# Moving LayerNorm tiles within SBUF by four transfers on one counter, in place of a round trip through DRAM, under a new order list

## The chip, the cores and the metric

The kernel runs on one core of a Trainium2 chip. The core has five engines with a queue of instructions each: TensorE (PE in the profile; its weight loads have a row of their own, PEld), VectorE (DVE), ScalarE (ACT), GpSimd (POOL) and SyncE (SP), which here only issues DMA transfers. The metric is the device time of one execution in microseconds, median of several runs; less is better.

## The reference, cut to what matters

Two transformer layers with shared weights on x of shape (1, 2048, 512) in bf16. Each layer is a sliding-window attention block and an MLP block, both with a LayerNorm in front and a residual behind:

```python
def _A_ref(x, wqkv, wo):                      # H = 32 heads of Dh = 16, window W = 256
    qkv = (x @ wqkv).reshape(B, S, 3, H, Dh).transpose(2, 0, 3, 1, 4)
    q, k, v = qkv[0], qkv[1], qkv[2]
    scores = einsum("bhqd,bhkd->bhqk", q, k) * (Dh ** -0.5)
    scores = where((i - j >= 0) & (i - j < W), scores, -1e9)
    return einsum("bhqk,bhkd->bhqd", softmax(scores), v) ... @ wo
def _B_ref(x, w1, b1, w2, b2):                # F = 1792
    return gelu_tanh(x @ w1 + b1) @ w2 + b2
for _ in range(2):
    x = x + _A_ref(_layernorm(x), wqkv, wo)
    x = x + _B_ref(_layernorm(x), w1, b1, w2, b2)
```

## The kernel before, in words

**Tiling.** The 2048 rows are 16 tiles of 128 rows; with the two layers there are 32 tiles, tau = 0 to 31. X stays in SBUF for the whole kernel. Attention works on blocks of two tiles (16 blocks, `attention(b, ...)`): scores of a block are computed in visits of 512 columns into four PSUM banks (line 944), ACT takes the exponential of them into the ring `E` (line 948), DVE or POOL multiplies the triangular parts with a mask (line 969), PE multiplies with V (line 1031), DVE transposes and scales the sums (lines 1034 to 1046), and PE applies Wo (`outproj`). The MLP works on ten jobs of two or four tiles (`mlp`, line 1091): W1 for 14 chunks of F, gelu on ACT (lines 1106 and 1114), W2, and the residual (line 790).

**LayerNorm and the transposed rows.** `layernorm` (line 727) computes the normalised rows of a tile on DVE and POOL (lines 734 to 747). PE needs them with the model dimension on the partitions. For early and for the last tiles, PE transposes them through PSUM (line 768). For 44 of the 64 LayerNorm tiles (`by_dma`: those in front of attention from tau = 14 on, those in front of the MLP from tau = 4 to 29) it goes another way: DVE transposes in blocks of 32 x 32 into one of four buffers `xs_` (line 753), SP writes that buffer to a scratch tensor `scr` in DRAM (line 758), and when that has landed, SP reads it back in another order into the destination (line 760): `xnTA` (18 tiles, read by the projections to Q, K and V) or `xnTB` (26 tiles, read by W1). Each transfer moves 128 KB; eight scratch buffers are used in turn.

**What sets the order.** Every operation is recorded as a node by `add` (line 200) with its engine, its reads and writes. `ORDER` is a list of all nodes, written out, found in advance by a search; `TURNS` says which engine takes an operation that two engines could do, `BANKS` which PSUM banks it gets. `_List.run` goes through `ORDER`, with planned durations; those of the two transfers are at lines 756 to 761. `_Sched.op` (line 89) then gives each operation its semaphore waits, and `emit` (line 164) writes each engine's instructions in the order of the list. So every engine runs a fixed queue. SP's queue holds the first loads, the 88 transfers of the LayerNorm tiles and the 17 stores of the result; a transfer that waits holds up all behind it. A transfer is counted on one of 16 DMA counters, used in turn; a transfer adds 16 to it when it has landed, and may be issued only when the counter's last one has landed (line 102).

Of the kernel before, what the change touches and what calls it, by code (L numbers as in the profile page):

```python
# [6 lines left out]
dt = mybir.dt  # L7
# [48 lines left out]
class _Sched:  # L56
# [32 lines left out]
    def op(self, eng, fn, reads=(), writes=(), inc=1, dma=False, start=0.0, end=0.0, n=1, joins=(), behind=None):  # L89
# [7 lines left out]
        counter = eng  # L97
        if dma:
            counter = "dma%d" % (self.dma_rr % self.N_DMA_SEMS)
            self.dma_rr += 1  # L100
            inc = 16
            need(counter, self.cnt_val[counter])
# [12 lines left out]
        waits = sorted(req.items(), key=lambda x: -self.when[x])  # L115
# [12 lines left out]
        self.prog[eng].append(dict(fn=fn, waits=waits, counter=counter, inc=inc, start=start, n=n))  # L128
# [35 lines left out]
    def emit(self):  # L164
        nc = self.nc
        self.spread()
        with nc.Block() as block:
            for eng in self.ENGINES:
                prog = self.prog[eng]

                def run(e, _prog=prog, _pe=eng == "pe"):
                    for o in _prog:
                        if _pe:
                            r = o["fn"](_Slots(e, o["at"]))
                        else:
                            for c, v in o["waits"]:
                                e.wait_ge(self.cnt_sem[c], v)
                            if o["fn"] is None:
                                continue
                            r = o["fn"](e)  # L180
                        r.then_inc(self.cnt_sem[o["counter"]], o["inc"])
# [4 lines left out]
class _List:  # L186
# [13 lines left out]
    def add(self, eng, fn, dur, reads=(), writes=(), prio=0.0, alloc=(), free=(), after=(), geo=None, table=None,  # L200
            issue=0.0, alt=(), war=(), lock=False, joins=()):
# [17 lines left out]
        if eng == "pe":  # L219
# [6 lines left out]
            issue=issue, lock=lock, alts=((eng, fn, dur),) + tuple(alt), n=n, behind=None,  # L226
# [72 lines left out]
def bass_interleave_layers__sliding_block__dense_activation_gelu__prompt_kernel(  # L299
# [44 lines left out]
    NSC = 8  # L344
# [30 lines left out]
    with ExitStack() as kctx:  # L375
        S_ = _Sched(nc, kctx)

        def sb(name, shape, dtype=dt.bfloat16):
# [20 lines left out]
        scr = nc.dram_tensor("scr_x", (NSC, P, D), dt.bfloat16, kind="Internal").ap()  # L399
# [811 lines left out]
```

## Time and profile before

| what | us |
|---|---|
| three runs, median | 448.97 (448.90 to 451.24) |
| the profiled execution's own time | 449.14 |
| its span, first to last instruction | 447.4 |
| PE, ACT, DVE, POOL busy | 425.2, 386.4, 373.5, 239.9 |

The profile is of one execution; its span is 1.7 us shorter than its time. An engine is busy while one of its instructions runs; matmuls are pipelined, so that two that overlap count once and a busy PE need not be at its peak. A "wait" is idle time of an engine and is put down to what ended it. DMA-issuing instructions are not busy time; for them the profile tells the time from issue to landing.

### The profile page before, as it was taken

What the parts mean: (1) busy time and instruction counts of PE and PEld (TensorE: products, weight loads), DVE (VectorE), ACT (ScalarE), POOL (GpSimd) and SP (SyncE); (2) the same over time, 40 slices, a digit from 0 to 9 for tenths busy, and PEclk for the clock granted to TensorE, in tenths of its full rate; (3) what the DMA queues carried; (4) which work ended last, traced back from release to release, by engine and by line L of the source; (5) the groups of instructions that cost most, each with busy time, mean ns of one, the idle gap of its engine ahead of it and who ended that gap; (6) DMA issues with size and microseconds to landing.
All of it is one profiled execution on the core that took longest, in us unless ns stands there. A gap on an engine that the chain in (4) does not pass through costs nothing.

```text
span 447.4 us, 19245 instructions
## 1 busy us (share of the span) xinstructions
PE 425.2 (95%) x8691; PEld 232.2 (52%) x8764; DVE 373.5 (83%) x745; ACT 386.4 (86%) x458; POOL 239.9 (54%) x301
## 2 busy tenths in 40 slices
PE   8999999888999999999999999999999999999997
PEld 5555655645544545545445445445454454545665
DVE  6999989899998989888999898998898876775512
ACT  2999999999999998899997999889979999892452
POOL 4764786755865357643356457672455454444330
DMA  9920000001120112010220101301031003002021
GB/s 264 370 88 4 4 1 3 5 3 50 43 56 13 50 51 75 25 37 16 68 67 3 39 24 50 74 15 49 27 85 50 15 5 94 22 8 62 0 84 48
DMA packets 39903, 22.88 MB, mean 51 GB/s; under 512 B 24460, under 2 KB 39308, under 8 KB 39820
## 3 DMA queue, kind: packets, MB, share of 16 engines
q1 hardware_dynamic: 39404, 21.24, 16.4%
q8 instruction: 69, 1.13, 1.0%
q10 hardware_dynamic: 416, 0.39, 0.3%
q14 instruction: 14, 0.11, 0.1%
HBM read 13.77 MB, written 7.86 MB: 48 GB/s over the span
## 4 chain that ended last, share of the span: by engine, by line
PE 70%; ACT 15%; DVE 10%; issue 2%; DMA 2%; POOL 0%
PE ps L32 69%; ACT E L948 10%; ACT gT L1114 2%; ACT gT L1106 2%; DVE TT L1034 2%; DVE E L969 1%; DMA xnTB<-scr_x 1%; DVE stat L734 1%; DVE QT L720 1%; ACT L948 1%; DVE X L790 1%; DVE xs_ L753 1%; DMA scr_x<-xs_ 1%; DVE Va L720 1%; DVE OT L1044 1%
## 5 line engine op out<-in xcount | busy, mean ns | idle before, releaser
L948 ACT ACTIVATE E<-ps 128x1024 bf16<-128x1024 f32 x304 | 285.7, 1044 | 23.9 <-PE ps L32 23.0
L969 POOL TENSOR_TENSOR E<-E,mask 128x512 bf16<-128x512 bf16 (+1 forms) x130 | 134.8, 1052 | 89.9 <-DVE E L969 40.8
L32 PE MATMUL ps<-xnTB,W_sb 128*128 128x512 bf16 (+1 forms) x560 | 115.2, 337 | 1.4 <-issue 0.3
L32 PE MATMUL ps<-W_sb,gT 128*128 128x512 bf16 (+1 forms) x421 | 108.4, 373 | 4.3 <-issue 3.0
L32 PE MATMUL ps<-xnTA,Wqkv_sb 128*128 128x256 bf16 (+1 forms) x544 | 74.6, 267 | 1.5 <-ACT E L948 0.7
L32 PEld LDWEIGHTS ps<-xnTB,W_sb 128*128 128x128 bf16 x560 | 51.6, 98 | 42.9 <-ACT E L948 3.8
L32 PE MATMUL ps<-QT,KT 32*64 32x320 bf16 (+4 forms) x2976 | 65.5, 258 | 4.0 <-ACT E L948 2.0
L790 DVE TENSOR_TENSOR X<-X,ps 128x512 bf16<-128x512 bf16 x63 | 42.4, 676 | 25.3 <-PE ps L32 25.0
L32 PEld LDWEIGHTS ps<-W_sb,gT 128*128 128x128 bf16 x462 | 41.5, 98 | 42.2 <-issue 6.7
L1114 ACT ACTIVATE gT<-ps,b1T 128x512 bf16<-128x512 f32 (+1 forms) x84 | 45.7, 598 | 20.1 <-PE ps L32 19.8
L32 PEld LDWEIGHTS ps<-xnTA,Wqkv_sb 128*128 128x128 bf16 x544 | 47.0, 98 | 24.2 <-ACT E L948 3.5
L32 PEld LDWEIGHTS ps<-QT,KT 32*64 32x64 bf16 x2976 | 27.6, 103 | 51.0 <-ACT E L948 32.5
L969 DVE TENSOR_TENSOR E<-E,mask 128x512 bf16<-128x512 bf16 (+1 forms) x132 | 49.1, 402 | 3.0 <-ACT E L948 3.0
L741 POOL TENSOR_TENSOR statmv<-statmv,mhalf 128x1 f32<-128x1 f32 x64 | 36.6, 575 | 22.8 <-DVE statmv L738 18.9
L32 PE MATMUL ps<-E,Va 64*17 64x128 bf16 (+3 forms) x3872 | 46.0, 229 | 2.5 <-ACT E L948 0.9
L1034 DVE STREAM_TRANSPOSE TT<-ps 128x1024 f32<-128x1024 f32 x32 | 39.8, 1244 | 9.4 <-PE ps L32 9.1
L32 PEld LDWEIGHTS ps<-E,Va 64*17 64x17 bf16 x3872 | 36.7, 85 | 19.5 <-PE ps L32 8.0
L1039 POOL TENSOR_TENSOR TM<-TT,Rc 128x512 bf16<-128x512 f32 x22 | 23.3, 1058 | 44.0 <-DVE E L969 17.8
L734 DVE BATCH_NORM_STATS2 stat<-X 128x6 f32<-128x512 bf16 x64 | 43.0, 678 | 2.7 <-DMA X<-in_A_x_dram 2.4
L1078 POOL TENSOR_TENSOR X<-X,b2b 128x512 bf16<-128x512 bf16 x32 | 36.7, 1157 | 13.2 <-DVE E L969 5.7
L1103 DVE TENSOR_SCALAR gT<-ps,b1T 128x512 bf16<-128x512 f32 (+1 forms) x56 | 35.5, 643 | 8.0 <-PE ps L32 7.7
L864 DVE TENSOR_TENSOR KT<-ps,parmask 128x1024 bf16<-128x1024 f32 x30 | 36.2, 1210 | 2.7 <-PE ps L32 2.5
(56 smaller groups left out, 348.5 us busy)
## 6 DMA issues: line engine op xcount, KB each, us to landing
scr_x<-xs_ SPq DMA_DIRECT2D x44, 128.0 KB, 1.9
W_sb<-in_B_w_dram SPq DMA_DIRECT2D x2, 1792.0 KB, 15.4
xnTB<-scr_x SPq DMA_DIRECT2D x26, 128.0 KB, 2.7
xnTA<-scr_x SPq DMA_DIRECT2D x18, 128.0 KB, 2.7
out_dram<-X SPq DMA_DIRECT2D x15, 128.0 KB, 1.8
Wqkv_sb<-in_A_wqkv_dram SPq DMA_DIRECT2D x4, 256.0 KB, 4.9
X<-in_A_x_dram SPq DMA_DIRECT2D x1, 1024.0 KB, 9.2
Wqkv_sb<-in_A_wqkv_dram SPq DMA_DIRECT2D x1, 512.0 KB, 6.4
```

The source lines that it names most:

```text
L32: return self.e.matmul(*a, **k)
L734: add("dve", lambda e, B: e.bn_stats(stat6[:, k6, :], X[:, t, :]), 590, reads=["X%d" % t], writes=["st%d" % k6], prio=prio)
L741: add("pool", lambda e, B: e.tensor_tensor(out=statmv[:, k, 1:2], in0=statmv[:, k, 1:2], in1=mhalf[:], op=ALU.pow), 535, reads=["ve%d" % k ...
L790: add("dve", lambda e, B: e.tensor_tensor(out=X[:, t, :], in0=X[:, t, :], in1=ps[:, B[g][0], :], op=ALU.add), d_psum(512), reads=["X%d" % ...
L864: add("dve", lambda e, B, g=g, i=i: e.tensor_tensor(out=KT[:, kb, :, 2 * i : 2 * i + 2, :].rearrange("p a c q -> p a (c q)"), in0=ps[:, B[ ...
L948: add("act", lambda e, B, g_=g_, gi=gi: e.activation(E[:, 2 * gi : 2 * gi + 2, e0 : e0 + 512], ps[:, B[g_][0] : B[g_][0] + 2, :], AF.Exp, ...
L969: op = lambda e, B, Ew=Ew, Mw=Mw: e.tensor_tensor(out=Ew, in0=Ew, in1=Mw, op=ALU.mult)
L1034: add("dve", lambda e, B: e.transpose(TT[:, s].rearrange("p a c q d -> p a (c q d)"), ps[:, B[g][0] : B[g][0] + 2, :].rearrange("p a n -> ...
L1039: mul = lambda e, B: e.tensor_tensor(out=TM[:, sm].rearrange("p c q a d -> p a (c q) d"), in0=TT[:, s, :, :, :, 0:Dh].rearrange("p a c q d ...
L1078: add("pool", lambda e, B: e.tensor_tensor(out=X[:, t, :], in0=X[:, t, :], in1=b2b[:], op=ALU.add), 1110, reads=["X%d" % t, "b2b"], writes ...
L1103: add("dve", lambda e, B, g=g, fc=fc: e.tensor_scalar(out=gT[:, fc, 0:M], in0=ps[:, B[g][0], 0:M], scalar1=b1T[:, fc : fc + 1], scalar2=No ...
L1114: add("act", lambda e, B, g=g, fc=fc: e.activation(gT[:, fc, 0:M], ps[:, B[g][0], 0:M], AF.Gelu_apprx_tanh, bias=b1T[:, fc : fc + 1], scal ...
```

## The change

For the 44 tiles the two transfers by way of DRAM become four transfers from SBUF to SBUF. Each takes 32 partitions of `xs_`, 32 KB, and writes 256 bytes to each of the 128 partitions of the destination. All four are issued one after another by SP and count on the same counter, which thereby rises by 64; the scratch tensor is gone. A node of the list can now consist of several transfers (`parts`).

```diff
@@ layernorm @@
-                flat = scr[v].rearrange("p c -> (p c)")
-                room = 0.0 if tau < 12 else 700.0
-                dma(lambda e, B: e.dma_start(scr[v], xs_[:, z, :]),
-                    ["scr%d_0" % v], reads=["xs%d" % z], prio=prio, dur=2200.0 + room, issue=400.0)
-                dma(lambda e, B: e.dma_start(dst.rearrange("p r d j -> p r (d j)"), flat.rearrange("(r p c) -> p r c", r=4, p=P)),
-                    [dname], reads=["scr%d_0" % v], prio=prio, dur=2700.0 + 2 * room, issue=400.0)
+                def move(e, B):
+                    return [e.dma_start(dst[:, r].rearrange("p d j -> p (d j)"), xs_[32 * r : 32 * r + 32, z, :].rearrange("i (q c) -> i q c", q=4))
+                            for r in range(4)]
+
+                dma(move, [dname], reads=["xs%d" % z], prio=prio, dur=4500.0, issue=1600.0, parts=4)
@@ _Sched.op @@
-            inc = 16
+            inc = 16 * parts
@@ _Sched.emit @@
-                        r.then_inc(self.cnt_sem[o["counter"]], o["inc"])
+                        for x in r if isinstance(r, list) else [r]:
+                            x.then_inc(self.cnt_sem[o["counter"]], o["inc"] // o["parts"])
```

`ORDER`, `TURNS` and `BANKS` are replaced as a whole. The new list has 3219 nodes in place of 3263. What can be counted in the two lists: PE issues 8766 matmuls in both, and changes between its three kinds of matmul (128 rows, scores, attention times V) 362 times before and 364 times after; ACT loads 18 tables in both, and the exponentials stand in the same groups between the gelus (44, 24, 50, 34, 1, 39, 40, 40 and 32). ACT takes over three copies of Q, two of V, one to `xnTA` and one to `xv`, and gives one to `xnTB` to DVE. Eight mask operations, three scalings of the attention's sums and one small operation move from POOL to DVE. SP issues 176 transfers for the LayerNorm tiles in place of 88.

More of the change, by code (lines that the diff above doesn't have):

```diff
@@ L87, in _acquire, with op @@
         return True
-    def op(self, eng, fn, reads=(), writes=(), inc=1, dma=False, start=0.0, end=0.0, n=1, joins=(), behind=None):
+    def op(self, eng, fn, reads=(), writes=(), inc=1, dma=False, start=0.0, end=0.0, n=1, joins=(), behind=None, parts=1):
         kn = self.know[eng]
@@ L127, in op @@
             self.res_r[wr] = {}
-        self.prog[eng].append(dict(fn=fn, waits=waits, counter=counter, inc=inc, start=start, n=n))
+        self.prog[eng].append(dict(fn=fn, waits=waits, counter=counter, inc=inc, start=start, n=n, parts=parts))
         return counter, val
@@ L200, in add @@
     def add(self, eng, fn, dur, reads=(), writes=(), prio=0.0, alloc=(), free=(), after=(), geo=None, table=None,
-            issue=0.0, alt=(), war=(), lock=False, joins=()):
+            issue=0.0, alt=(), war=(), lock=False, joins=(), parts=1):
         i = len(self.nodes)
@@ L225, in add @@
             jdeps=frozenset(self.lw[r] for r in joins), alloc=alloc, free=tuple(free), deps=deps, geo=geo, table=table,
-            issue=issue, lock=lock, alts=((eng, fn, dur),) + tuple(alt), n=n, behind=None,
+            issue=issue, lock=lock, alts=((eng, fn, dur),) + tuple(alt), n=n, behind=None, parts=parts,
             heavy=any(a[0] == "pool" and a[2] > 600.0 for a in ((eng, fn, dur),) + tuple(alt)),
@@ L343, in bass_interleave_layers__sliding_block__dense_activation_gelu__prompt_kernel @@
     NXV = 1
-    NSC = 8
     LN_DMA = 14
@@ L398, in bass_interleave_layers__sliding_block__dense_activation_gelu__prompt_kernel @@
         b1raw = xv[0:FC, 0, 0, :]
-        scr = nc.dram_tensor("scr_x", (NSC, P, D), dt.bfloat16, kind="Internal").ap()
         xnTA = sb("xnTA", [P, 2, 2, DC * P])
@@ L680, in bass_interleave_layers__sliding_block__dense_activation_gelu__prompt_kernel, with dma @@
             add("pe", clear(n), took, reads=["zero", "g0"], writes=["ps:init0", "ps:init1"], prio=-200, geo="f")
-        def dma(fn, writes, reads=(), dur=2200.0, prio=0.0, issue=640.0, eng="sp"):
-            add(eng, fn, dur, reads=reads, writes=writes, prio=prio, issue=issue)
+        def dma(fn, writes, reads=(), dur=2200.0, prio=0.0, issue=640.0, eng="sp", parts=1):
+            add(eng, fn, dur, reads=reads, writes=writes, prio=prio, issue=issue, parts=parts)
         queued = {"sp": 0, "act": 0}
@@ L750, in layernorm @@
                 z = xs_rr[0] % NXS
-                v = xs_rr[0] % NSC
                 xs_rr[0] += 1
@@ L1179, in bass_interleave_layers__sliding_block__dense_activation_gelu__prompt_kernel @@
             marks[i] = S_.op(nd["eng"], lambda e, fn=nd["fn"]: fn(e, B), reads=phys(nd["reads"]), writes=phys(nd["writes"]), dma=nd["issue"] > 0,
-                  start=nd["start"], end=nd["vis"], n=n, joins=nd["joins"], behind=marks[nd["behind"]])
+                  start=nd["start"], end=nd["vis"], n=n, joins=nd["joins"], behind=marks[nd["behind"]], parts=nd["parts"])
         S_.wait_all_dma("sp")
```

419 rows, old and new, of tables (BANKS, ORDER, TURNS) are left out of this document.

## The prediction

> **What bounds the kernel now.** I read the page's first part, then the table of stages, the waits, and last the transfers with SP's timeline.
>
> ```profile
> span 447.4 us, 19245 instructions
> PE 425.2 (95%) x8691; PEld 232.2 (52%) x8764; DVE 373.5 (83%) x745; ACT 386.4 (86%) x458; POOL 239.9 (54%) x301
> ```
>
> The share hides two regimes; the stages tell them apart.
>
> ```profile
> 13.00:49.00 36.00, 32.59 (x789) 18.64 (x792) 34.42 (x72) 35.42 (x39) 23.64 (x34) 1.00 0.37 126
> ...
> 85.00:124.00 39.00, 35.27 (x889) 21.04 (x892) 36.63 (x73) 38.61 (x47) 26.67 (x29) 1.00 0.11 30
> 124.00:160.00 36.00, 35.38 (x742) 17.54 (x753) 33.07 (x68) 35.15 (x41) 16.77 (x21) 1.00 0.14 36
> 160.00:200.00 40.00, 39.00 (x840) 20.58 (x829) 34.76 (x69) 36.27 (x42) 26.03 (x33) 1.00 0.17 45
> 200.00:240.00 40.00, 38.94 (x763) 19.70 (x770) 36.64 (x74) 36.60 (x42) 16.72 (x19) 1.00 0.19 49
> 240.00:285.00 45.00, 43.43 (x1001) 22.23 (x1010) 41.07 (x84) 42.64 (x49) 27.62 (x37) 1.00 0.14 37
> 285.00:320.00 35.00, 33.94 (x596) 17.27 (x585) 31.82 (x60) 31.84 (x39) 17.55 (x23) 1.00 0.14 37
> 320.00:360.00 40.00, 38.87 (x816) 20.82 (x823) 34.26 (x62) 36.05 (x42) 20.49 (x21) 1.00 0.17 45
> 360.00:400.00 40.00, 38.90 (x857) 19.03 (x864) 30.52 (x57) 35.56 (x39) 17.39 (x21) 1.00 0.13 36
> ```
>
> The columns are length, then PE, PEld, DVE, ACT, POOL busy, the granted clock, the DMA share and GB/s. From 13 to 124 us ACT is all but full (35.42 of 36, 38.61 of 39) and PE waits. From 124 to 400 us it is the other way round: PE lacks only 0.62 + 1.00 + 1.06 + 1.57 + 1.06 + 1.13 + 1.10 = 7.5 us, ACT about a tenth. The first LayerNorm tile that a transfer moves is transposed at 100 us, so the change works where PE sets the pace, and 7.5 us is the most that filling PE's visible idle time could give there.
>
> ```profile
> PEld ps L32 <- ACT E L948: 46.9, 130, 0.8
> ...
> PEld ps L32 <- DMA xnTB<-scr_x: 0.8, 1, 0.8
> ```
>
> In the waits of all engines a transfer holds up the weight loads once, for 0.8 us; the banks that the exponentials empty do so 130 times. The transfers are nearly hidden already.
>
> **The change part by part.** *Removed: the write to DRAM and the read back.*
>
> ```profile
> L758 SPq DMA_DIRECT2D scr_x<-xs_ x44: 319/332/914, 100.7 to 407.9; - x44
> ...
> scr_x<-xs_ SPq DMA_DIRECT2D x44, 128.0 KB, 1.9
> ...
> xnTB<-scr_x SPq DMA_DIRECT2D x26, 128.0 KB, 2.7
> xnTA<-scr_x SPq DMA_DIRECT2D x18, 128.0 KB, 2.7
> ...
> out_dram<-X SPq DMA_DIRECT2D x2, 64.0 KB, 1.5
> ```
>
> ```profile
> 100.71 0.34 SPq L758 DMA_DIRECT2D scr_x<-xs_  x1
> 102.42 0.38 SPq L760 DMA_DIRECT2D xnTB<-scr_x  x1
> ...
> 308.09 1.04 SPq L758 DMA_DIRECT2D scr_x<-xs_  x2
> 310.56 0.92 SPq L760 DMA_DIRECT2D xnTA<-scr_x  x2
> ```
>
> In the window of that last pair, and over all 88 transfers, issue to landing was:
>
> ```profile
> DMA to landing us min/median/max: 2.2/2.4/2.7
> ```
>
> ```profile
> DMA to landing us min/median/max: 1.7/2.3/4.1
> ```
>
> A lone tile's read is issued 1.71 us after its write (102.42 − 100.71) and lands 2.7 us later: 4.4 us. For two tiles together the second read goes out about 0.46 us after 310.56 and lands at 313.7, 5.6 us after the first write.
>
> *Added: four 32 KB transfers a tile, 176 in all.* No row shows a transfer from chip to chip. Back to back an issue takes 0.46 us (two reads in 0.92). A landing is bounded below by 1.5 us (64 KB to DRAM) and above by 2.7 (128 KB in the same 256-byte pieces); I take 1.9, the row of the write, whose source is the same tile. A lone tile then needs 3 × 0.46 + 1.9 = 3.3 us (bounds 2.9 and 4.1), 1.1 less than now; a pair 7 × 0.46 + 1.9 = 5.1, 0.5 less. SP now issues 176 × 0.46 = 81 us in place of 44 × (0.33 + 0.46) = 35.
>
> ```profile
> SPq L758 <- DVE xs_ L753: 217.2, 20, 80.9
> ...
> SPq L760 <- DMA scr_x<-xs_: 32.4, 20, 3.6
> SPq L760 <- PE ps L32: 6.0, 2, 4.1
> ```
>
> SP's own waits show what hides that: it stands 217 us waiting for DVE's transposes. The 32.4 us behind its own writes go. The wait for PE to release `xnTA` stays; what queues behind it are the four transfers and whatever tile follows on SP. Without that cover each tile would cost its successor 1.0 us more of issue. The four `xs_` buffers are held 3.3 us in place of 1.9; DVE then waits only if four tiles fall within that time, so nothing. The reader waits for 64 on one counter in place of 16, and a counter comes round after 16 tiles in place of 8: nothing.
>
> *Gained directly.* The one stall is at the start of an MLP job:
>
> ```profile
> 280.89 3.70 DMA scr_x<-xs_
> ...
> 284.60 4.20 DMA xnTB<-scr_x
> ...
> 288.84 1.41 PEld L32 LDWEIGHTS ps<-xnTB,W_sb 128*128 128x128 bf16 x8 [0.80 <-DMA xnTB<-scr_x]
> ```
>
> Here both moves were slow, 7.9 us in place of 4.4, and PE lost 0.8. I take −0.8.
>
> *Lost: the new list leaves less room.* In both order lists I priced the PE work that stands between a tile's transpose and the first PE instruction that reads it, the tightest tile for each of 17 readers.
>
> ```profile
> 402.49 3.40 PE L32 MATMUL ps<-W_sb,gT 128*128 128x512 bf16 x15
> ...
> 279.90 0.42 PE L32 MATMUL ps<-QT,KT 32*64 32x256 bf16 x16
> ...
> 281.81 0.74 PE L32 MATMUL ps<-E,Va 64*17 64x64 bf16 x64
> ...
> L753 DVE STREAM_TRANSPOSE xs_<-xn x44: 653/702/712, 100.0 to 407.2; 128x512 bf16<-128x512 bf16 x44
> ```
>
> Fifteen matmuls in 3.40 us, of which the last one's own 0.38 is drain, make 0.216 us for each of 512 columns; 0.108 for 256, 0.42 for a score visit, 0.74 for half an attention-times-V. The shortest rooms before: 6.8, 7.0, 7.0, 8.1, 8.8 us. After: 3.0 (14 second-MLP matmuls, tile 29), 4.3, 4.3, 4.9, 5.3, 5.9, then 7.1 and more. Needed are 0.70 of transpose and 3.3 = 4.0: one reader is short, by 1.0 us. With a last landing of 4.1, the slowest above, it would be 6.2 and six readers short, by 9.5 in sum. The list is no clock either: the stalled tile had 7.0 listed, and 288.84 − 280.89 + 0.70 = 8.7 with its stall. I take +2.0, near the lower end since most landings are near their median, bounds 0 and 9.5.
>
> *The rest of the list.* PE issues 8766 matmuls in both; it changes between the three array shapes 364 times in place of 362, +0.3 us by the small idle times at such a change (bounds 0 and 0.8). ACT loads 18 tables in both.
>
> ```profile
> L722 ACT ACTIVATE Va<-ps 128x512 bf16<-128x512 f32 x7 | 4.3, 611 | 0.0
> L722 ACT ACTIVATE QT<-ps 128x512 bf16<-128x512 f32 (+1 forms) x9 | 4.3, 508 | 2.6 <-PE ps L32 2.6
> L878 ACT ACTIVATE xv<-xnTA 128x512 bf16<-128x512 bf16 x4 | 2.6, 639 | 0.0
> ...
> L969 POOL TENSOR_TENSOR E<-E,mask 128x512 bf16<-128x512 bf16 (+1 forms) x130 | 134.8, 1052 | 89.9 <-DVE E L969 40.8 <-DVE xn L744 26.7 <-ACT E L948 11.8
> ```
>
> ```profile
> L948 ACT ACTIVATE E<-ps x128: 1017/1042/1155, 12.8 to 159.2; 128x1024 bf16<-128x1024 f32 x128
> ```
>
> ACT gets three more copies to QT, two to Va and one to `xv`; one xnTA copy more and one xnTB copy fewer cancel: 3 × 0.508 + 2 × 0.611 + 0.639 = 3.4 us. Between the first and the 128th exponential, 12.8 to 159.2 us, both lists give it three copies; one more stands ahead of the first, the rest falls where ACT has a tenth to spare. Cost nothing; with that cover gone, 3.4. POOL gives eleven large operations (1.05 us each) to DVE, an engine that is not the bound here; DVE gives up six copies for them.
>
> *Gained by the order itself.* What an earlier landing lets the order pack is bounded by 0 and the 7.5 us of PE idle; nothing in the rows fixes it. I take −2.0, nearer to nothing, because transfers held PE up for only 0.8 us.
>
> Sum, on the profiled execution's own 449.14 (span 447.4 and 1.7 around it; the median of three, 448.97, is 0.2 lower): 449.14 − 0.8 + 2.0 + 0.3 − 2.0 = 448.6, or **448.5** against the median.
>
> **The rivals.** *Slower: the rooms are too short.* The point of decision is a need of about 5 us from transpose start to landing. At 5.1 (0.7 + 4.4, no faster than a lone tile before) four readers are short by 3.9 in sum, at 6.2 six by 9.5; with the old stall gone, the shape changes added and nothing gained by the order, 449.1 − 0.8 + 0.3 + 3.9 = 452.5 to 458.1; the middle, 455. For it: six rooms of 3.0 to 5.9 us where before none was under 6.8. Against it: one landing in place of two for each tile.
>
> *Faster: the order fills PE.* If half of the 7.5 us is filled and no room is too short: 449.1 − 0.8 − 3.8 = 444.5. For it: SP's 32.4 us behind its own writes vanish, with every tile behind them. Against it: PE's matmuls and shape changes are the same, and PE has only those 7.5 us to give.
>
> *The change does not shorten the move.* If the four moved one after another, four landings of 1.9 make 7.6, with the transpose 8.3: nine readers are short by 24.3 in sum: 449.1 − 0.8 + 0.3 + 24.3 = 473. It decides as soon as the fourth landing follows the first by more than the three issues. The trace speaks against it: the two reads issued 0.46 apart at 310.56 landed 2.2 and 2.7 after their issues, no slower than one alone. [...]
>
> **How the numbers follow.** 0.5%, 2.2 us, is about what a measurement of this kernel can tell from no change. Within it (446.7 to 451.2): 0.38, the likeliest. Slower by short rooms: 0.28; by transfers in series: 0.05; together 0.33. Faster: 0.29. The range 443.5 to 456.5 takes in the faster rival and most of the slower; about 0.1 lies beyond each end. The forecast's own range is 446.7 to 451.2.
>
> **What would show it.** Right: four issues in some 1.8 us and the last landing 3 to 3.5 us after the first issue; one or two waits of the weight loads on the transfers, 1 to 2 us in sum; 124 to 400 us as full on PE as now. Wrong towards slower: several such waits, most at the starts of MLP jobs with the short rooms, or landings over 4 us. Wrong towards faster: PE's idle time in those stages under 4 us. Wrong in my view of the start: the stages before 100 us, which no transfer touches, longer or shorter by over 1 us.

## The result, and the profile after

| | before | after |
|---|---|---|
| median of the runs, us | 448.99 (448.90 to 451.24) | 455.49 (454.83 to 458.00) |
| the profiled execution, its span | 449.14, 447.4 | 454.83, 453.0 |
| from HBM, to HBM, MB | 13.77, 7.86 | 8.00, 2.10 |

The ratio is 1.0141, 95% interval 1.0102 to 1.0181: slower by 6.5 us, where 448.5 was forecast. The page of the changed kernel begins:

```profile
span 453.0 us, 19327 instructions
## 1 busy us (share of the span) xinstructions
PE 424.9 (94%) x8688; PEld 231.4 (51%) x8764; DVE 375.4 (83%) x751; ACT 389.2 (86%) x464; POOL 231.1 (51%) x289
```

PE is as busy as before, in a span 5.6 us longer: it has no more to do, it waits more. One caution for the stages: the profiles before and after hold 8691 and 8688 of the 8766 matmuls, those of most kernels below all but two, and a record that is missing seems to show as a short idle time of PE. From 49 to 85 us PE is busy for 33.34 us here and for 34.34 in the first kernel below, with the same work, so a microsecond in a stage says nothing. The stages (length, PE, PEld, DVE, ACT, POOL busy, granted clock, DMA share, GB/s) say where:

```profile
85.00:124.00 39.00, 34.71 (x881) 20.00 (x885) 36.62 (x76) 38.06 (x46) 22.27 (x32) 1.00 0.09 16
124.00:160.00 36.00, 34.28 (x687) 17.27 (x692) 31.30 (x61) 33.88 (x39) 19.07 (x22) 1.00 0.09 16
160.00:200.00 40.00, 35.65 (x848) 18.75 (x855) 32.30 (x68) 31.68 (x36) 19.04 (x25) 0.96 0.14 24
200.00:240.00 40.00, 39.05 (x708) 19.45 (x714) 36.58 (x72) 38.87 (x45) 20.31 (x24) 1.00 0.15 28
...
360.00:400.00 40.00, 38.84 (x864) 19.61 (x870) 31.10 (x54) 36.53 (x43) 16.66 (x19) 1.00 0.15 36
```

One stage stands out: between 160 and 200 us PE was busy 39.00 of 40 before and is 35.65 now, and for the first time a granted clock is under 1. Counting exponentials dates it more finely. The 304 are the same work in both lists, so the start of the k-th can be compared: after minus before is −1.0 us for the 81st (102 us), +1.3 for the 113th (135 us), +0.4 for the 145th (178 us), +5.6 for the 161st (215 us), and stays between +4.4 and +6.0 to the end. So the stages ahead of the first transfer won a microsecond, 100 to 135 us lost two, and one place between 178 and 215 us lost five.

Before the place, the price of the transfers. The rows of the instructions that use `xs_` give count, issue time min/median/max in ns, and the landing:

```profile
L752 SPq DMA_DIRECT2D xnTB<-xs_ x104: 542/603/1958, 105.7 to 419.0; - x104
L752 SPq DMA_DIRECT2D xnTA<-xs_ x72: 543/604/1467, 125.4 to 345.6; - x72
...
DMA to landing us min/median/max: 1.9/2.0/3.6
```

A transfer lands 2.0 us after its issue, as estimated (1.9). But an issue takes 0.60 us, not 0.46, and 24 of the 176 took over 0.9. The four issues of a tile take 3.07 us in the median (2.48 to 3.91; I took 1.84), and from a tile's first issue to its last landing 4.7 us pass (3.8 to 6.2; I took 3.3). SP's queue and DVE's transposes around the place, then PE:

```profile
165.55 12.14 SPq L752 DMA_DIRECT2D xnTB<-xs_  x11
177.73 3.29 SPq L752 DMA_DIRECT2D xnTA<-xs_  x4
181.07 3.29 SPq L752 DMA_DIRECT2D xnTB<-xs_  x4
```

```profile
165.90 1.28 DVE L748 STREAM_TRANSPOSE xs_<-xn 128x512 bf16<-128x512 bf16 x2
173.37 0.65 DVE L748 STREAM_TRANSPOSE xs_<-xn 128x512 bf16<-128x512 bf16 x1
176.97 0.70 DVE L748 STREAM_TRANSPOSE xs_<-xn 128x512 bf16<-128x512 bf16 x1
```

```profile
181.32 1.48 PE L32 MATMUL ps<-xnTA,Wqkv_sb 128*128 128x256 bf16 x12
185.75 0.60 PE L32 MATMUL ps<-xnTB,W_sb 128*128 128x512 bf16 x2 [2.96 <-DMA xnTB<-xs_]
```

The last of the four tiles that the fourth MLP job reads is transposed at 177.68. At that moment SP begins the four issues of another tile, one for `xnTA` that was transposed by 167.2 and that nobody reads before 193.7. They take 3.29 us. Only then, at 181.07, come the four issues of the urgent tile; the last lands at 185.71, and PE goes on at 185.75 after 2.96 us of nothing. Of the 8.0 us from transpose to landing, 3.4 are the neighbour's.

In windows of 2 us around it the third figure from the end is the granted clock:

```profile
182.00:184.00 2.00, 0.80 (x8) 0.47 (x6) 1.63 (x6) 1.49 (x2) 0.86 (x3) 1.00 0.22 41
184.00:186.00 2.00, 0.24 (x2) 0.13 (x3) 0.42 (x1) 0.00 (x0) 1.58 (x2) 1.00 0.18 33
186.00:188.00 2.00, 1.67 (x29) 0.76 (x29) 1.22 (x1) 0.66 (x1) 0.00 (x0) 0.59 0.00 0
188.00:190.00 2.00, 2.00 (x7) 0.74 (x6) 0.00 (x0) 1.27 (x2) 0.00 (x0) 0.56 0.00 0
190.00:192.00 2.00, 2.00 (x33) 0.84 (x32) 1.19 (x2) 0.79 (x1) 0.00 (x0) 1.00 0.00 0
```

PE stands still from 182.80 to 185.75, and runs at half clock from 186.34 on for 3.41 us: 7 matmuls in two microseconds. That is up to 1.7 us of work lost (an estimate, half of the 3.41) on top of the 2.96, together 4.7 of the five.

The long issues have a partner in the trace: the transfers that the page lists as a queue of the kind `instruction`.

```profile
q8 instruction: 69, 1.13, 1.1%
```

These are 69 transfers of 16 KB, 0.88 to 1.50 us long; I call them fetches. That they bring in PE's program is an estimate from the counts, since no view tells whose they are: PE has two instructions for each of the 8766 matmuls, 17532 in a page of 19327, and 17532 / 69 = 254 would come with each. Each of the 24 long issues runs while a fetch is under way, and ends 0.28 to 0.40 us after it; in the kernel before, where 4 of SP's 88 issues for the LayerNorm tiles took over 0.9 us, it is 4 of 4, and 0.36 to 0.42 us. Of the change's 152 shorter ones 132 meet no fetch, and 18 of the other 20 had been running for 0.29 us or more when it began. Three long issues stand in the row that ends with the stall, at 174.63, 179.04 and 182.36; beyond 0.60 us each they add 2.6 us, nearly as much as PE's 2.96. So an issue seems to wait for the fetch; by what means, the trace does not show.

### The profile page after: what moved, and what is told of

Read it like the earlier page. It is cut to its first block, busy times and chain, and to the rows that moved or that the text cites. A ratio compares the mean times of both kernels' runs of the same rounds, so it can differ in the third digit from the quotient of the medians.

```text
span 453.0 us, 19327 instructions
## 1 busy us (share of the span) xinstructions
PE 424.9 (94%) x8688; PEld 231.4 (51%) x8764; DVE 375.4 (83%) x751; ACT 389.2 (86%) x464; POOL 231.1 (51%) x289
## 4 chain that ended last, share of the span: by engine, by line
PE 58%; ACT 23%; DVE 10%; DMA 3%; issue 2%; SPq 2%
PE ps L32 58%; ACT E L942 16%; ACT gT L1108 3%; ACT gT L1100 2%; DMA xnTB<-xs_ 2%; SPq L752 2%; DVE E L963 2%; DVE TT L1028 1%; DVE KT L858 1%; DVE xs_ L748 1%; ACT L1100 1%; ACT L942 1%; DVE X L784 1%; DVE stat L730 1%; DVE OT L1038 1%
## 5 line engine op out<-in xcount | busy, mean ns | idle before, releaser
L963 POOL TENSOR_TENSOR E<-E,mask 128x512 bf16<-128x512 bf16 (+1 forms) x122 | 129.3, 1075 | 106.8 <-DVE E L963 51.3
L32 PE MATMUL ps<-W_sb,gT 128*128 128x512 bf16 (+1 forms) x420 | 110.0, 373 | 4.6 <-issue 4.3
L963 DVE TENSOR_TENSOR E<-E,mask 128x512 bf16<-128x512 bf16 (+1 forms) x140 | 56.6, 433 | 3.7 <-ACT E L942 3.4
L32 PE MATMUL ps<-Wo_sb,OT 128*128 128x512 bf16 x112 | 32.6, 379 | 1.7 <-issue 0.6
```

What stands on the lines that cost most here:

```text
L32: return self.e.matmul(*a, **k)
L963: op = lambda e, B, Ew=Ew, Mw=Mw: e.tensor_tensor(out=Ew, in0=Ew, in1=Mw, op=ALU.mult)
```

## The experiments

**The theory**: SP's serial issues are the price. What counts is a tile's own four and those of a neighbour that stand in front; the new list itself costs nothing. **The rivals**: the list is to blame (its short rooms); the shape of the transfers (256-byte pieces) is; or split moves run in series. All ratios are to the kernel before, on the same chip.

**One tile's place.** The four issues of the unhurried `xnTA` tile go behind those of the urgent one; nothing else is changed.

```diff
+        ORDER.remove(1314)
+        ORDER.insert(ORDER.index(1156) + 1, 1314)
```

> The changed kernel with one node of its order list moved: the four transfers of the xnTA tile that SP issued at 177.7 us now stand behind those of the xnTB tile that SP issued at 181.1 us and that PE waited for until 185.75 us. Theory (SP's issue time and its queue made one tile late, PE stood 3.0 us and then ran 3.4 us at half clock): the tile lands about 3.3 us earlier, the stall and the half clock go, and the time is 455.5 - 3.0 - 1.7 = about 450.5. Rival (the new list loses its time everywhere, or the landings are slow as such): one tile changes nothing, 455.

Measured: 451.85 us, ratio 1.0044 (1.0026 to 1.0063). The urgent tile's issues begin at 177.87 and land at 182.71; its reader starts at 182.76 without a stall, and no clock is under 1:

```profile
160.00:200.00 40.00, 40.00 (x902) 20.69 (x881) 36.55 (x79) 36.42 (x41) 21.27 (x28) 1.00 0.14 25
```

So one swap in SP's queue was worth 0.97%, 4.4 us. What is left, 2 us against before, is in part smaller waits of the same kind, 1.7 us of PE's in sum, the longest at the MLP job near 290 us:

```profile
PE ps L32 <- DMA xnTB<-xs_: 1.2, 1, 1.2
```

**How many issues a tile.** Three kernels keep the list, the bytes and the waits, and move a tile by one, two or four copies from partitions to the same partitions. This is not the LayerNorm tile that is wanted: rows and columns land in other places. The added lines are, in turn, for one, two and four.

```diff
-                    return [e.dma_start(dst[:, r].rearrange("p d j -> p (d j)"), xs_[32 * r : 32 * r + 32, z, :].rearrange("i (q c) -> i q c", q=4))
-                            for r in range(4)]
+                    return [e.dma_start(dst.rearrange("p r d j -> p (r d j)"), xs_[:, z, :])]
+                    return [e.dma_start(dst[64 * h : 64 * h + 64].rearrange("p r d j -> p (r d j)"), xs_[64 * h : 64 * h + 64, z, :])
+                            for h in range(2)]
+                    return [e.dma_start(dst[32 * r : 32 * r + 32].rearrange("p r d j -> p (r d j)"), xs_[32 * r : 32 * r + 32, z, :])
+                            for r in range(4)]
```

> The changed kernel and its list with one transfer of 128 KB a tile in place of four; rows and columns go to other places than the computation needs, the bytes and the list are the same. Theory (issue time on SP): one issue of 0.4 to 0.6 us a tile, landing about 2 to 2.7 us later, no stall at the third MLP job; the list then shows what it is worth: 449 or up to 2 us less. Rival (the list): 455.

> Leaves out: as in the run with four plain copies, a moved tile lands in other places than the readers want; here by two transfers of 64 partitions. With one transfer the same list took 448.0 us, with four 455.5. By the theory (SP's queue is charged for every issue, and only tiles whose neighbour's issues stand in front are late): two issues take 1.0 to 1.3 us, the tile that stalled by 3.0 us comes 1.9 to 2.4 us earlier than with four and stalls by 1.1 us at most, no granted clock under 1, and 448.5 to 450.5 us. By the rival (a move that is split over disjoint partitions runs in series, so that two halves are already as slow as four quarters): the last landing follows the first by 1.5 us or more beyond the issue's distance, and 453 us or more.

> Leaves out: the transfers only copy partitions to the same partitions, so that rows and columns of a moved tile land in places where the readers do not want them; the number of transfers, their bytes, the waits and the list are those of the changed kernel. Question: does an issue cost 0.60 us because of what the transfer does (32 partitions spread over 128 in 256-byte pieces) or because it is one more transfer? By the theory (the four issues in SP's queue are the price, whatever their shape): issue 0.55 to 0.65 us, four of them 2.4 us or more, the stall near 186 us stays at 1.5 us or more, and the time is 453 to 457 us. By the rival (the spreading makes the issue slow, and a plain copy of 1 KB rows is issued in 0.33 to 0.46 us, as one whole tile was in 0.46): four issues in 1.9 us or less, no stall over 0.5 us at 186 us, and 448.5 to 451 us.

| transfers a tile | us | ratio (95%) |
|---|---|---|
| one of 128 KB | 448.04 | 0.9966 (0.9952 to 0.9979) |
| two of 64 KB | 448.46 | 0.9983 (0.9971 to 0.9994) |
| four of 32 KB, plain | 455.08 | 1.0125 (1.0094 to 1.0155) |
| four of 32 KB, the change | 455.49 | 1.0141 (1.0102 to 1.0181) |

The rows of `xs_` with one, two and four, each kernel for itself:

```profile
L752 SPq DMA_DIRECT2D xnTB<-xs_ x26: 464/465/612, 105.8 to 410.2; - x26
...
DMA to landing us min/median/max: 1.9/2.1/3.9
```

```profile
L752 SPq DMA_DIRECT2D xnTB<-xs_ x52: 461/597/1795, 105.8 to 410.8; - x52
...
DMA to landing us min/median/max: 1.9/2.1/3.9
```

```profile
L752 SPq DMA_DIRECT2D xnTB<-xs_ x104: 507/591/1866, 105.9 to 419.6; - x104
...
DMA to landing us min/median/max: 1.8/1.9/3.8
```

Landing takes 1.9 to 2.1 us in the median, for the three sizes and for both shapes. With one transfer an issue is 0.46 us; with two, the first takes 0.46 and the one right behind it 0.60 (medians). The four plain copies take 0.59 each and reproduce the loss, with a stall of 3.21 us at the same place and half clock from 187 us on: not the pieces, not the spreading over partitions, but the number of issues. And the price does not grow evenly with their number. By the ratios it is 0.8 us from one to two, and 6.4 from two to four. With two, the `xnTA` tile is out of SP's queue before the urgent one is transposed; with four it is not. The long issues grow in number too: over 0.9 us are 2 of 44 with one, 10 of 88 with two and 24 of 176 with four. The first row is also the value of the list with one short transfer a tile: 1.5 us better than before.

**The old list with four transfers.** The other half of the change alone: `ORDER`, `TURNS` and `BANKS` are those of before, and the four transfers stand where the write stood, or behind the last reader of their destination; a DVE transpose whose buffer is not yet read moves back behind the transfers that free it.

```diff
+                key[i] = max(key[d] for d in nd["deps"] | {i - 1}) + 0.5
+        ORDER.sort(key=key.get)
```

> The order list of before with the four transfers: the write's node does nothing, the four transfers stand where the write stood, or behind the last reader of the destination if that is later; one DVE transpose is moved back behind the transfers that free its buffer. Theory (the cost of four issues is paid only where a reader has little room; the old list's rooms are 6.8 us and more): 449 to 450. Rival (transfers from chip to chip are slower for any list): 453 or more. Rival (the list alone is at fault): 449 as well; told apart from the theory by the run with one issue.

Measured: 463.74 us, ratio 1.0303 (1.0284 to 1.0322), not what the theory said. The rows of `xs_` show another wait that the four transfers bring:

```profile
its engine sat idle before it (us, times) until:
  DMA xnTB<-xs_: 7.9, 5
  DMA xnTA<-xs_: 4.5, 1
```

DVE stands 12.3 us because its four buffers are not free; PE stands 4.7 us in one piece behind the longest of these waits, and runs at half clock for 6.8 us. By way of DRAM, `xs_` came free when the write had landed, 1.9 us after its issue, and the tile waited for its place in eight scratch buffers; now it waits in `xs_` itself. To take that away, 16 tiles whose buffer is wanted soon keep the way by DRAM in the next kernel:

```diff
+                if (xs_rr[0] - 1) in KEEP:
+                    dma(lambda e, B: e.dma_start(scr[v], xs_[:, z, :]),
+                        ["scr%d_0" % v], reads=["xs%d" % z], prio=prio, dur=2200.0, issue=400.0)
+                    dma(lambda e, B: e.dma_start(dst.rearrange("p r d j -> p r (d j)"), flat.rearrange("(r p c) -> p r c", r=4, p=P)),
+                        [dname], reads=["scr%d_0" % v], prio=prio, dur=2700.0, issue=400.0)
+                    return
```

> The order list of before. 28 of the 44 tiles take the four transfers, issued where the list had the write or after the last reader of the room they go to; the other 16, whose buffer is wanted again soon (in the earlier run with the old list DVE stood waiting for just these buffers), keep the write to DRAM and the read back. By the theory (the old list's rooms, none under 6.8 us, cover a tile that takes 0.7 us of transpose, 2.5 to 3.3 of issue and 2 of landing; what cost 14 us in the earlier run was the buffers): DVE waits for a transfer by less than 1 us in sum, PE waits for transfers by 2 us at most, and 448.5 to 451 us. By the rival (the four issues are too dear under any list, the new list is not to blame): PE's waits for transfers of 3 us or more, and 453 us or more.

Measured: 457.33 us, ratio 1.0178 (1.0147 to 1.0209): the rival's side, with a stall of 1.9 us and a half clock behind it. DVE still waited 2.7 us for its buffers, where I had said less than 1, so not all of the loss is the issues'. SP's queue ahead of it:

```profile
222.02 1.90 SPq L766 DMA_DIRECT2D xnTA<-xs_  x3
223.97 0.59 SPq L759 DMA_DIRECT2D scr_x<-xs_  x1
226.85 0.38 SPq L761 DMA_DIRECT2D xnTB<-scr_x  x1
227.27 2.49 SPq L766 DMA_DIRECT2D xnTA<-xs_  x4
229.80 3.42 SPq L766 DMA_DIRECT2D xnTB<-xs_  x4
233.64 0.38 SPq L761 DMA_DIRECT2D xnTB<-scr_x  x1
234.07 2.48 SPq L766 DMA_DIRECT2D xnTB<-xs_  x4
```

```profile
238.74 1.89 PE L32 MATMUL ps<-xnTB,W_sb 128*128 128x512 bf16 x4 [1.87 <-DMA xnTB<-xs_]
```

SP is hardly idle from 226.85 to 236.55, and the four of the tile that PE waits for come last. At this stall the issues are too dear for the old list as well; my hope that rooms of 6.8 us and more would cover them left out the neighbours again.

**The new list with the old route.** The converse: write and read back under the changed kernel's list, the write where the four stood, the read twelve places later in the list (`a` and `b` keep it behind the last reader of its destination and ahead of its own).

```diff
+                reads.setdefault(order[min(max(at[i] + 12, a), b - 1)], []).append(i)
```

> The order list of the changed kernel with the transfers of before: at the place of the four transfers stands the write to DRAM, and the read back follows some two microseconds later in the list. So far: this list with one transfer a tile 448.0 us, with two 448.5, with four 455.5. By the theory (SP's time per tile and the need of the tight tiles decide, and the list itself is worth a microsecond): SP spends 0.33 + 0.40 us on issues of a tile in place of 3 and the buffers come free after 2 us, but a lone tile still needs 4.4 us from the first issue to the landing, as much as with four; so tiles behind a neighbour are early and lone tight tiles as late as in the changed kernel: no stall of PE over 1.5 us, no half clock, and 448.3 to 451 us. By the rival (the list was drawn up for a move with one landing, and two landings one after the other fit it worse than four issues): stalls at the MLP jobs with the short rooms, and 453 us or more.

Measured: 458.81 us, ratio 1.0208 (1.0156 to 1.0260); the theory's 448.3 to 451 failed, and so did its "no half clock": there is one at 186.63. Its waits:

```profile
PE ps L32 <- DMA xnTB<-scr_x: 5.7, 3, 2.7
PEld ps L32 <- DMA xnTB<-scr_x: 3.6, 3, 3.0
```

So the new list did well only with a short move: one landing and few issues (448.0). Given two landings in a row it loses 9 us, given four issues 6.5. The twelve places were one choice, and SP stood 56.6 us behind its own writes in place of 32.4; that no other place for the reads would do better is not shown. Neither list can be judged without its transfers.

**Two queues.** On the list with the one tile moved, ACT issues two of the four transfers of the ten tightest tiles; in the first kernel ACT's two stand where SP's stood, in the second right behind the transpose.

```diff
+            if i in shared:
+                for eng, rs, mark in (("sp", (0, 1), ""), ("act", (2, 3), "~")):
+                    marks[i] = S_.op(eng, lambda e, fn=nd["fn"], rs=rs: fn(e, B, rs), reads=phys(nd["reads"]), writes=[nd["writes"][0] + mark],
+                                     dma=True, start=nd["start"], end=nd["vis"], parts=2)
```

> The list of the changed kernel with the one tile's transfers moved behind its neighbour's (451.85 us in the earlier run); of the ten tiles that landed last before their readers, two of the four transfers are issued by ACT in place of SP. By the theory (SP's serial issues, not the transfers' own time, make the tiles late): the ten tiles land 0.8 to 1.5 us sooner after their transposes, the stall of 1.4 us at the MLP job near 290 us is under 0.5, and the time is 449 to 450.7 us. By the rival (issues of two queues, or the transfers themselves, share one resource): the landings come no sooner, and 451.5 us or more. A third way: the issues and their waits stand in ACT's stream ahead of exponentials, and ACT's delay shows in the waits of the weight loads on the exponentials; then 452 us or more with sooner landings.

> As the earlier run in which ACT issued two of the four transfers of ten tiles; there ACT's issues stood as late in ACT's stream as SP's in SP's, up to 4 us behind the transpose, so that it told nothing of two queues. Here ACT's two stand right behind the transpose. By the theory (SP's serial issues make the tiles late): ACT's halves land before SP's, the tight tiles 0.8 us or more sooner than with SP alone (451.85 us), no stall over 1.2 us, and 449.5 to 451.5 us. By the rival (two queues share one resource): landings no sooner than with SP alone. Against both: ACT, which is nine tenths busy, may stand waiting for a transpose that its stream reaches early, and every microsecond of that comes back on PE through the exponentials; then 453 us or more, with ACT's waits for the transposes to show it.

Measured: 462.43 us, ratio 1.0294 (1.0273 to 1.0316), and 470.27, ratio 1.0466 (1.0418 to 1.0514). In the first, ACT's issues came up to 7.4 us behind the transpose, since they stood behind ACT's other work. In the second, two queues did what the theory says: seven of the ten tiles have every landing on record both here and with SP alone, and in all seven the last came sooner behind the transpose, by 1.0 to 2.9 us. Here is one transposed at 423.53, whose last transfer landed at 426.4, 2.8 us after the first issue (4.7 is the median with SP alone).

```profile
423.56 1.20 SPq L754 DMA_DIRECT2D xnTB<-xs_  x2
```

```profile
418.31 1.27 ACT L1110 ACTIVATE gT<-ps,b1T 128x512 bf16<-128x512 f32 x2
423.56 1.47 ACTq L754 DMA_DIRECT2D xnTB<-xs_  x2
425.08 1.27 ACT L1110 ACTIVATE gT<-ps,b1T 128x512 bf16<-128x512 f32 x2 [5.50 <-issue]
```

```profile
426.40 1.99 PE L32 MATMUL ps<-E,Va 64*17 64x64 bf16 x104 [4.03 <-ACT gT L1110]
```

But ACT had stood 4 us waiting for that transpose, PE then 4.03 for ACT. So the issues of two queues did not hold each other up here, 1.20 us on SP and 1.47 on ACT side by side; a busy engine's queue is no place for a transfer that waits.

**Filling PE's gap.** To price the half clock, 24 matmuls whose result is thrown away go ahead of the job that stalled.

```diff
+                    for _ in range(24 if again else 0):
+                        e.matmul(ps[:, B[g][0], part[0][2]], part[0][0], part[0][1], start=True, stop=True)
```

> The changed kernel with 24 extra matmuls of 256 columns (thrown away) on PE just ahead of the wait that ended at 185.75 us: 24 x 0.108 = 2.6 of the 3.0 us are filled, the transfer lands when it did. Theory (the idle time itself makes the clock fall to half for 3.4 us): the stall stays but the granted clock stays at 1.00, 1.7 us less than the changed kernel, 453.8. Rival (the clock falls for another reason, such as the work after the stall): no change, 455.5.

Measured: 464.57 us, ratio 1.0332 (1.0294 to 1.0370). Where it was put it worked: the gap was 0.24 us in place of 2.96, and the clock was full. But far behind it PE paused in the middle of groups, for no data, and three half clocks followed:

```profile
262.31 0.35 PE L32 MATMUL ps<-E,Va 64*17 64x128 bf16 x16 [2.08 <-issue]
```

It tells nothing of the clock's price, but asks a question of its own: do 48 more PE instructions (24 matmuls, 24 weight loads) harm because of their number? Two kernels put one-column matmuls into the warm-up instead, the second 128 in place of 24. With 128 they are 256 instructions, about the 254 of one fetch: if PE pauses where the share of one fetch ends, which is an estimate of mine, a shift by about one share leaves the pauses where they were.

```diff
+                for b in [0] * (24 if n == 8 else 0):
+                    e.matmul(ps[:, b, 0:1], gT[:, 0, 0:P], zero[:, 0:1], start=True, stop=True)
```

> The changed kernel with 24 one-column matmuls more in the warm-up, 48 PE instructions, about 2.5 us before the first data arrives and so for nothing. In the run that filled PE's gap with 24 extra matmuls, PE later stood still three times for some 2 us in the middle of a group, put down to issue and to no data, each followed by a half clock, and the run lost 8 us there. By the theory (every later PE instruction stands 48 places further along, and PE pauses where its program is fetched; the order list is fitted to where these pauses fall): pauses of about 2 us put down to issue appear here too, with the 3.0 us stall of the changed kernel still there, and 458 us or more. By the rival (the extra matmuls where they stood, not the shift, made those pauses): no pause put down to issue over 1 us, and 454 to 457 us.

> As the run with 24 one-column matmuls more in the warm-up (468.2 us against 455.5 for the changed kernel; PE paused eleven times by up to 2.0 us for no data, 12.6 us in sum), but with 128 of them, a shift of 256 PE instructions. The 24 took 1.0 us at the start, so 128 put the first exponential off by 5.4 us, to some 18 us. [...] By the rival (any shift, or the extra matmuls themselves, make the pauses): 450 us or more from the first exponential to the end, as with 24 (453.2), and 468 us or more.

Measured: 468.17 us, ratio 1.0416 (1.0378 to 1.0453), with 24, and 458.95, ratio 1.0205 (1.0155 to 1.0254), with 128. PE's waits for no data in the first (in the kernel with the one tile moved, whose profile lacks as few matmuls, 1.4 us in two waits), then the first and last start of its exponentials and of those of the second:

```profile
PE ps L32 <- issue: 12.6, 11, 2.0
```

```profile
L944 ACT ACTIVATE E<-ps x304: 1017/1030/1163, 13.5 to 415.2; 128x1024 bf16<-128x1024 f32 x152
```

```profile
L944 ACT ACTIVATE E<-ps x304: 1018/1032/1192, 16.0 to 406.0; 128x1024 bf16<-128x1024 f32 x152
```

From the first exponential to the last the changed kernel takes 388.7 us (12.46 to 401.16), with 24 more 401.7, with 128 more 389.9. Five times as many added instructions cost almost nothing in between. The first exponential stood at 16.0 and not at 18; from there to the end are 441.5 us, against 440.5 in the changed kernel (453.0 − 12.46) and the 450 or more of the rival. With 128 more, no wait of PE for no data is over 1.0 us (8.3 us in 44 waits, in a profile that lacks 79 matmuls). So PE can stand up to 2.08 us for no data, and how many instructions stand ahead matters. That the pauses fall where the share of a fetch ends agrees with these runs, but they do not show it. The traces before and after have one pause each for no data over 0.3 us behind the warm-up at full clock: 0.31 us up to 27.57 before, 0.74 up to 80.89 after. They ended 1.38 and 1.26 us after a fetch. `_List.run` plans the list's durations with such pauses (`CODE`).

The kernel with one transfer a tile runs the PE program of the change and shows no loss, so such pauses of PE are no part of the 6.5 us. They are the reason why the fill-in run can't be read.

## Why the prediction was wrong, step by step

**What bounds the kernel**: right, PE paces from 124 us on. But the 7.5 us of idle time that bounded what the order could gain were in good part none: the profile before lacks 75 matmuls, and with two transfers a tile, where two are missing, PE's busy times in the same stages fall 0.4 us short of full.

**"Back to back an issue takes 0.46 us"**: the step that failed. The row was two reads from DRAM; the change's copies are issued in 0.54 when they come alone, in 0.60 right behind another, and about every seventh, met by a fetch, in 1.1 to 2.0. SP's issues came to 125.7 us in place of 81. At 0.46, an estimate, the stall would not have come: the tile issued from 174.05 on and the unhurried one behind it would have kept SP until 174.05 + 8 × 0.46 = 177.7, just when the urgent tile was transposed.

**"A lone tile needs 3 × 0.46 + 1.9 = 3.3 us"**: 4.7 in the median, of which the landing, 2.0, was right and the issues were not. With 0.70 of transpose that is 5.4, past the point of about 5 us at which I let the slower rival decide.

**"SP's own waits show what hides that"**: failed with it. SP still waits for DVE:

```profile
SPq L752 <- DVE xn L740: 114.4, 7, 86.1
SPq L752 <- DVE xs_ L748: 52.8, 5, 16.1
SPq L752 <- PE ps L32: 47.6, 4, 23.6
```

But that is a few long waits (86.1 of 114.4 us in one). The issues come in bunches, up to four tiles are begun within twelve microseconds, and there is no cover inside a bunch. I had priced what happens without it at 1.0 us a tile; at the tile that stalled it was 3.4.

**"I take +2.0, bounds 0 and 9.5"** for the rooms: the term that was mis-sized. With 1.0141 after and 0.9966 for the same list with one issue, the four issues cost 1.75%, 7.9 us: 4.4 by the one tile that was moved, 3.5 by the rest, of which PE's remaining waits for transfers are 1.7. The rooms themselves were right: the tile that stalled has 5.3 us listed and took 8.7 from transpose start to landing, short by 3.4; PE stood 2.96.

**The half clock**, up to 1.7 us, stood in no term.

**`xs_` held longer: "nothing"**: right under the new list, where DVE waited 1.3 us for it, and wrong as a reason: under the old list it was 12.3.

**Gained directly, order and shape changes**, −0.8 − 2.0 + 0.3 = −2.5: with one transfer the same list gave −1.5. The sum is near; no run tells its three terms apart, nor what ACT's and POOL's changed operations cost. The 0.3 is two changes of shape at the 0.16 us for which PE stood idle at some of them before:

```profile
169.25 0.81 PE L32 MATMUL ps<-Wqkv_sb,xv 128*128 128x512 bf16 x3 [0.16 <-issue]
```

**The rivals.** "Slower: the rooms are too short", 452.5 to 458.1, middle 455, is what happened, by a need of 5.4 us and more. Its need came from dearer issues and neighbours, not from a landing as slow as before. That its middle met the 455.5 is luck: it counted four to six short readers, while 4.4 of the loss hang on one reader, and 1.7 of those on a clock that it left out. The moves did not run in series: each of four lands 2.0 us after its own issue, and the kernel with two halves took 448.46 us, the one with one whole 448.04. It is the issues that stand in a row: one takes 0.60 us beside 2.0 of landing, the four of a tile 3.07.

**What stays open**: why an issue on SP is held up while a fetch is under way, and the 1.8 us of the loss that are in no wait of PE for a transfer. No version that beats both kernels came of it: the kernels at 448.0 and 448.5 move partitions only onto themselves, and the spreading that the readers need was not done with fewer than four transfers here.

## What to carry to other kernels

A transfer cost its issuing queue once for each issue here, 0.46 us for 128 KB as for 64 and 0.54 for 32, so splitting a move by four multiplied the scarce part, and the chances of meeting a fetch (24 of 176 issues over 0.9 us, 4 of 88 before). Don't set an engine's total idle time against its new work: for each reader with little room, write down what stands ahead of its transfer in the queue, and order that queue by deadline. When a list was drawn up for one kind of transfer, keep list and transfers together, and keep the number of matrix instructions, before a run with one of them changed is read.

## What the runs showed of the hardware

- **Half clock behind a stall of PE.** In the changed kernel the half clock begins at 186.34, 0.59 us after the stall of 2.96 us has ended, and lasts 3.41 us. Stalls of 3.21 us (four plain copies), 2.73 (128 matmuls more), 2.68 (the new list with the old route) and 1.87 (16 tiles by way of DRAM) were followed by half clock as well, the one of 4.7 (the old list) by 6.8 us of it. In the kernel before, with the one tile moved, and with one or two copies a tile, no wait of PE was over 1.2 us and no granted clock under 1 in any stage. The length of a stall alone does not settle it: 2.10 us up to 135.04, with ACT's issues where SP's stood, and 2.5 us from 240.25 on, the new list with the old route, left the clock of their stages at 1.00.
- **More PE instructions, other pauses**: from the first exponential to the last 48 more cost 13.0 us, 256 more 1.2 (401.7 and 389.9 in place of 388.7).
- **A fetch and a long issue on SP go together**: of the issues over 0.9 us for the LayerNorm tiles 24 of 24 in the changed kernel and 4 of 4 in the one before met a fetch, and ended 0.28 to 0.42 us after it.
- **Issue times on SP**, medians: 0.33 us for 128 KB to DRAM (the kernel before); within SBUF, when it comes alone, 0.46 for 128 or 64 KB (one and two copies a tile) and 0.54 for the change's 32 KB, 0.60 right behind another; on ACT 0.61 to 0.74 (the two kernels with two queues).
